# An attention and convolution kernel on one core: its order of work, planned by a scheduler or written out as a list

## The chip, the cores and the metric

The kernel runs on one core of a Trainium2 chip. The core has a matrix engine (PE, with a separate queue for loading weights, PEld), a vector engine (DVE), a scalar engine (ACT), a general engine (POOL) and a queue engine (SP) that here only issues DMA transfers. Each engine works through its own instruction list in order and waits on semaphores for the others. Products land in PSUM, eight banks of 128 partitions by 512 floats, and everything else lives in SBUF.

The metric is the device time of one execution, in microseconds (us), as the median of several runs. Before the change it is 368.91 us (three runs: 368.1, 368.91 and 369.94).

## The reference

The computation has two halves. The first is attention in which a query only sees keys of its own cluster: q, k and v have 4 batches, 8 heads, 768 rows of 64 columns, and each head has 16 centroids.

```python
q_assign = np.argmax(np.einsum('bhsd,hcd->bhsc', q_n, c_n), axis=-1)   # q_n, c_n: rows of length 1
k_assign = np.argmax(np.einsum('bhsd,hcd->bhsc', k_n, c_n), axis=-1)
mask = q_assign[:, :, :, None] == k_assign[:, :, None, :]
scores = np.where(mask, scale * np.matmul(q, k.transpose(0, 1, 3, 2)), -1000000000.0)
attn = np.exp(scores - np.max(scores, axis=-1, keepdims=True))
attn = attn / (np.sum(attn, axis=-1, keepdims=True) + 1e-09)
attn_out = np.matmul(attn, v)
```

Its output, with the heads side by side as x of 4 batches, 768 rows and 512 columns, goes through a gated long convolution:

```python
proj = x @ w_proj
x1, x2, x3 = (proj[..., :D], proj[..., D:2 * D], proj[..., 2 * D:])
x2_conv = np.fft.irfft(np.fft.rfft(x2, n=S, axis=1) * np.fft.rfft(filter_fft, n=S, axis=0)[None], n=S, axis=1)
return (x1 * x2_conv * x3) @ w_out
```

## The kernel before, in words

**Two steps: plan, then emit.** `build` first records the whole kernel as 1987 operations with `Plan.op`. An operation names the engines that may do it with a duration for each, a due time, the keys that it reads and writes (from which its dependencies follow), the PSUM bank that it opens (`alloc`) and those that it releases (`free`). Then `Plan.place` decides for every operation its engine, its place in time and its bank. Last, a loop at the end of the kernel function goes through the resulting list and calls each operation's function, which emits the instructions. So an engine's instruction list is the planned list, cut down to that engine.

**What the planner goes by.** `place` (L124 to L238) keeps for every engine the time at which it is free and its operations whose dependencies are placed. It takes the engine that can start earliest and on it, among the operations that could start within 0.1 us of the first, the one with the least due time. It models DMA rates (`RATE`), the exp table's load (`TABLE`) and a lock that keeps DVE and POOL from doing certain operations at once (`lock`). Two tables correct it by hand: `NUDGE` (L43) adds an offset to the due time of nearly every operation, and `ONLY` (L44) pins some operations to one engine. Banks come from `banks_for` (L241 to L263): those that are free earliest by the planner's clock, with at most four (`HELD`) held by scores and four by everything else while scores are open; banks 4 and 5 belong to the output of the attention.

**Attention.** A group is four heads of one batch, so there are eight groups, each with two pairs of heads (`attention(n, pr)`), and a pair has six key tiles of 128: 96 tiles in all. For one tile PE makes three score products into three banks (`sc`, L700, through `product` at L80), ACT takes exp of each into a buffer p (L714 and L717, five buffers), and PE multiplies p by v (`pv`, L728), adding into banks 4 and 5 over the six tiles. DVE adds up p over the tiles (`acc`, L741; the first two tiles with `part`, L737, on DVE or POOL) for the denominators. The mask needs no separate pass: q and k, in bfloat16 buffers `augs`, carry 16 extra rows with the one-hot word of the cluster, so the score product itself lowers the scores of other clusters. Casting q and k into `augs` (L633; the copy itself is at L283 for ACT, L285 for DVE and POOL) can be done by ACT, DVE or POOL.

**Routing.** `routing(n)` prepares a group while the one before is in its attention: PE transposes q and k (L627) or DVE does (L605), PE makes the similarities to the centroids (`sim`, L647), DVE finds the greatest and its word (L652 to L662), PE turns the words into hits with a triangular matrix `tri` (L667), ACT or DVE copies them to `ohT` (L673, L675), and SP moves them with eight DMAs into the extra rows of `augs` (`masks`, L512). For the first group, which has nothing to hide behind, `first_masks` (L517) writes the rows of one pair from PSUM directly (`put`, L564).

**Start.** Ahead of the first score stand the centroids' norms (a square root on ACT, L357, and a Newton step on DVE, L360 to L365), the filter's angles (sines on ACT), zero fills of `augs` (L1087 on ACT, or POOL), and the loads of q and k, which SP and ACT issue (L331).

**Convolution.** After the second group of a batch, `hyena(b)` runs on the batch's 768 rows beside the attention of the following groups; only the last batch's lies behind all attention. Its products on PE are the spectral input U (L855), the spectrum (L483), the gates G (L917), the inverse I (L946) and the output product W, with DVE, ACT and POOL in between.

**Shape of the array.** `product` (L80) makes a product either with the whole array, or as two matmuls on halves of 64 columns. `array(o, last)` (L59) says which shape an operation needs: pv and some others 64, small ones 32, and scores, gates and inverses take the shape that came last.

**The lock.** In the emission loop, an operation marked `lock` that goes to POOL waits for the last such operation that the loop has emitted for DVE:

```python
if o.lock and o.on == "POOL" and held:
    tc.add_manual_dep(traced[n], held[0].name, ...)
elif o.lock and o.on == "DVE":
    held = [traced[-1]]
```

## Time and profile before

| | |
|---|---|
| median of 3 runs | 368.91 us |
| span of the profiled execution | 367.2 us |
| PE busy | 354.3 us (96%) |
| DVE busy | 341.4 us (93%) |
| ACT busy | 264.3 us (72%) |
| POOL busy | 125.2 us (34%) |
| granted PE clock | 9 or more tenths in every slice |
| DMA | 46.20 MB, mean 126 GB/s |
| first pv starts | 26.39 us |
| last accumulation starts | 320.2 us |

The span is the stretch from the first to the last recorded instruction of one profiled execution; the profile gives no other time for that execution, and the median of the runs is 1.7 us longer than the span. "Busy" is the time in which an engine has an instruction in work; a matmul that waits in PE's pipe for its operands counts as busy. The chain of waits is the path that ends last: it starts at the last instruction and goes back, at each step, to what released it.

### The profile page before, as it was taken

How to read it: one execution, taken by the hardware profiler on the slowest of the kernel's cores; microseconds unless marked ns; L12 is line 12 of the kernel's file. 1: busy time of each engine (PE TensorE's matmuls, PEld its weight loads, DVE VectorE, ACT ScalarE, POOL GpSimd, SP SyncE). 2: the span in 40 equal slices, each digit the busy share in tenths (PEclk: the TensorE clock that was granted, in tenths of full speed). 3: DMA queues.
4: the chain of work that ended last, by engine and by line, in shares of the span. 5: the costliest groups of instructions: out<-in, count | busy, mean ns of one | idle time of the engine just before them, and what ended most of it. 6: DMA issues, size and time to landing. Idle time of an engine off the chain costs nothing.

```text
span 367.2 us, 8472 instructions
## 1 busy us (share of the span) xinstructions
PE 354.3 (96%) x3201; PEld 205.5 (56%) x3204; DVE 341.4 (93%) x455; ACT 264.3 (72%) x500; POOL 125.2 (34%) x152
## 2 busy tenths in 40 slices
PE   7799999999999999999999999989999999999995
PEld 3456455445655554655555655568655655656662
DVE  5999898999999989999999999999997999999984
ACT  4999997768986876879699774759965796234342
POOL 7510515322003556221310056424021433126750
PEclk9999999999999999999999999999999999999999
DMA  7866996585667986857777898554357631110124
GB/s 165 193 153 141 192 188 154 112 182 99 147 139 129 149 153 110 164 121 103 140 99 142 223 192 162 98 103 89 60 90 195 127 37 43 45 46 3 59 116 172
DMA packets 109797, 46.20 MB, mean 126 GB/s; under 512 B 97640, under 2 KB 103484, under 8 KB 109756
## 3 DMA queue, kind: packets, MB, share of 16 engines
q1 hardware_dynamic: 104556, 35.07, 43.1%
q0 software_dynamic: 2752, 8.98, 16.8%
q10 hardware_dynamic: 2448, 1.61, 1.4%
q8 instruction: 25, 0.41, 0.5%
q14 instruction: 16, 0.13, 0.1%
HBM read 31.59 MB, written 7.40 MB: 106 GB/s over the span
## 4 chain that ended last, share of the span: by engine, by line
PE 74%; DVE 9%; ACT 6%; DMA 5%; issue 2%; SPq 1%; ACTq 0%; DVEq 0%
PE bank L85 31%; PE pair L728 29%; PE bank L855 6%; DVE acc L741 2%; PE bank L627 2%; ACT p L717 2%; PE bank L647 2%; PE bank L83 2%; DMA y<-in_moe_filter_fft_dram 2%; DMA aug<-ohT 1%; DMA qkraw<-in_q_dram 1%; PE bank L490 1%; ACT aug L283 1%; DVE qkP L285 1%; DVE hm L470 1%
## 5 line engine op out<-in xcount | busy, mean ns | idle before, releaser
L728 PE MATMUL pair<-p,vraw 128*64 128x385 f32 x768 | 144.5, 489 | 0.8 <-ACT osb L744 0.3
L717 ACT ACTIVATE p<-bank 128x512 f32<-128x512 f32 x192 | 108.9, 607 | 23.7 <-PE bank L85 16.9
L741 DVE TENSOR_TENSOR acc<-p,acc 128x1536 f32<-128x1536 f32 x64 | 112.8, 1762 | 3.3 <-ACT p L717 0.6
L728 PEld LDWEIGHTS pair<-p,vraw 128*64 128x64 f32 x768 | 58.7, 136 | 45.2 <-issue 35.0
L85 PE MATMUL bank<-aug,aug 128*64 128x256 bf16 (+3 forms) x728 | 81.8, 327 | 1.6 <-ACT p L717 0.6
L85 PEld LDWEIGHTS <-aug 80*64 80x64 bf16 (+1 forms) x728 | 47.5, 109 | 38.0 <-issue 24.5
L714 ACT ACTIVATE p<-bank 128x512 f32<-128x512 f32 x96 | 57.7, 605 | 6.2 <-PE bank L85 4.1
L774 POOL DMA_DIRECT2D acc<-acc x30 | 23.7, 798 | 84.4 <-DVE acc L741 57.1
L285 POOL CAST aug<-qkP 64x768 bf16<-64x768 f32 x22 | 19.6, 894 | 74.8 <-DVE acc L741 52.1
L85 PE MATMUL bank<-xT,wpj 128*64 128x384 bf16 x456 | 43.5, 326 | 0.3 <-ACT ohT L673 0.2
L85 PEld LDWEIGHTS <-wpj 128*64 128x64 bf16 x456 | 28.1, 110 | 12.5 <-issue 3.8
L85 PEld LDWEIGHTS <-y 128*64 128x64 bf16 x472 | 24.4, 110 | 16.0 <-issue 6.0
L737 POOL TENSOR_TENSOR acc<-p,p 128x1536 f32<-128x1536 f32 x7 | 24.3, 3466 | 18.9 <-ACT p L717 9.5
L885 DVE TENSOR_TENSOR tm<-bank,hm 128x512 f32<-128x512 f32 x44 | 28.4, 684 | 2.3 <-PE bank L490 1.1
L283 ACT CAST aug<-qkP 64x768 bf16<-64x768 f32 x28 | 23.1, 831 | 3.9 <-DVE qkP L605 1.8
L85 PE MATMUL bank<-wout,y 128*64 128x512 bf16 (+1 forms) x200 | 24.3, 371 | 0.9 <-DVE y L977 0.4
L855 PE MATMUL bank<-wpj,xT 128*64 128x512 bf16 x192 | 22.5, 379 | 0.0
L283 ACT COPY ob<-bank 128x512 f32<-128x512 f32 x21 | 12.0, 591 | 12.4 <-PE bank L85 11.7
L889 POOL TENSOR_TENSOR y<-tm 128x512 bf16<-128x512 f32 x14 | 17.7, 1276 | 8.7 <-DVE tm L885 4.4
L283 ACT COPY qkP<-bank 128x384 f32<-128x384 f32 x36 | 16.5, 485 | 5.6 <-PE bank L647 2.1
L977 POOL TENSOR_TENSOR y<-yy,x 128x768 bf16<-128x768 f32 x6 | 10.9, 1824 | 24.6 <-DVE yy L972 12.6
L627 PE MATMUL bank<-ident,qkraw 128*128 128x128 f32 x120 | 18.8, 281 | 0.4 <-DMA qkraw<-in_k_dram 0.3
(182 smaller groups left out, 451.7 us busy)
## 6 DMA issues: line engine op xcount, KB each, us to landing
qkraw<-in_q_dram SPq DMA_DIRECT2D x30, 192.0 KB, 4.5
rb<-dr SPq DMA_DIRECT2D x30, 192.0 KB, 3.5
qkraw<-in_k_dram SPq DMA_DIRECT2D x51, 96.0 KB, 2.8
vraw<-in_v_dram SPq DMA_DIRECT2D x48, 96.0 KB, 3.2
out_dram<-ob SPq DMA_DIRECT2D x9, 512.0 KB, 3.7
acc<-acc POOLq DMA_DIRECT2D x10, 384.0 KB, 5.2
acc<-acc POOLq DMA_DIRECT2D x10, 192.0 KB, 4.0
vraw<-in_v_dram SPq DMA_DIRECT2D x4, 384.0 KB, 4.3
```

Source lines behind the costliest of these rows:

```text
L85: T.nc.tensor.matmul(out[64 * i:64 * i + 64], lhsT[:, 64 * i:64 * i + 64], rhs, start=start, stop=stop)
L283: T.nc.scalar.copy(out, in_)
L285: (T.nc.vector if e == "DVE" else T.nc.gpsimd).tensor_copy(out, in_)
L627: T.nc.tensor.transpose(ap(h)[:, ts(t, 128)], raw(s, 3 * ch + t), T.ident[:, ::-1] if ch > j else T.ident)
L714: T.nc.scalar.activation(o, ap(h).rearrange("p (a b) -> p a b", a=2), Act.Exp, scale=0.125)
L717: T.nc.scalar.activation(flat(s)[:, lo:lo + 512], ap(h), Act.Exp, scale=0.125)
L728: T.nc.tensor.matmul(o[64 * hp:64 * hp + 64, ch, :385], T.vraw[vs][:, hp, sk * D:(sk + 1) * D], T.p[slots[sk]][:, hp, 384 * ch:384 * ch + ...
L737: alu(e).tensor_tensor(T.acc[os], T.p[slots[0]][:, :, :S], T.p[slots[1]][:, :, :S], op=Alu.add)
L741: T.nc.vector.tensor_tensor(T.acc[os], T.p[slots[sk]][:, :, :S], T.acc[os], op=Alu.add)
L774: op(("POOL", .8), lambda e, rows=rows: T.nc.gpsimd.dma_start(flat_()[:rows], flat_()[rows:2 * rows], accum_op=Alu.add), te, r=[], w=AK, b ...
L855: T.nc.tensor.matmul(ap(h)[64 * i:64 * i + 64], T.xT[xs][:, kt, c:c + 64], T.wpj[:, kt, DM:2 * DM], start=kt == 0, stop=kt == ND - 1)
L885: op(("DVE", .68), lambda e, i=i, cs=cs, r=r, h=h: T.nc.vector.tensor_tensor(T.tm[r][:, cs], ap(h), hmrow(i, (0, 2, 2, 3)[2 * r + cs]), op ...
```

## The change

`NUDGE`, `ONLY`, `place`, `banks_for`, the heap import and the planner's constants are removed. In their place stands `ORDER`, a list of 1987 numbers: each is five times an operation's index plus the index of its engine in `ENGINES`. A new method `arrange` goes through the list. It asserts that every operation stands behind what it depends on, sets its engine, and gives it the PSUM banks that have been free longest (first in, first out), where before the planner gave those that it expected to be free earliest. The limit of four held banks is gone. Banks 4 and 5 stay with the attention's output while that runs, and may be taken by others before (class "head", until the first score) and after it. The recorded operations, the functions that emit them, the emission loop and the lock in it are the same. The list puts the operations in a different order on every engine and some of them on another engine:

| operations | PE | ACT | DVE | POOL | SP |
|---|---|---|---|---|---|
| before | 634 | 505 | 439 | 116 | 293 |
| after | 634 | 519 | 428 | 111 | 295 |

Among them are the casts into `augs` (ACT 28 to 37, DVE 14 to 8, POOL 22 to 19), the first addition of a pair `part` (POOL 7 to 5, DVE 9 to 11), one copy `put` of the first masks and two zero fills, which leave ACT. Neighbours in the list are not neighbours in time: runs of one engine's operations stand together. After the change a line of code has a number some 39 lower; the prediction uses the numbers of before.

```diff
-HELD = 4
 EARLY = 8.73655
-NUDGE = {0:3.939,1:2.28,2:2.825,
...
-ONLY = {15:"POOL",16:"ACT",17:"POOL",
...
+ENGINES = ['PE', 'ACT', 'DVE', 'POOL', 'SP']
+ORDER = [
+    2, 13, 48, 103, 23, 18, 28, 106, 199, 174, 194, 189, 154, 201, 51, 66, 181, 169, 179, 149, 159, 5, 112, 117, 37, 267, 62, 122, 207, 237, 242,
...
+]
...
-        o.due += NUDGE.get(o.seq, 0.0)
...
-    def place(self, free0, banks_for, switch=0.1, wait=0.1, rate=RATE, bonus=0.0, margin=0.02195, shape=0.0):
...
+    def arrange(self):
+
+        free, last, outs, done = [0, 1, 2, 3, 6, 7, 4, 5], None, 0, set()
+        tiles = sum(o.alloc is not None and o.alloc.cls == "o" for o in self.ops)
+        closed, scores, order = 0, 0, []
+        for x in ORDER:
+            o = self.ops[x // 5]
+            o.on = ENGINES[x % 5]
+            assert o.on in o.eng and o.deps <= done and o not in done
+            done.add(o)
+            order.append(o)
+            if o.alloc is not None:
+                if o.alloc.cls == "o":
+                    ids, outs = [4, 5], outs + 1
+                else:
+                    right = closed == tiles if outs else o.alloc.cls == "head" and not scores
+                    ids = [i for i in free if right or i not in (4, 5)][:o.alloc.n]
+                scores += o.alloc.cls == "score"
+                assert len(ids) == o.alloc.n and set(ids) <= set(free)
+                o.alloc.ids = tuple(ids)
+                free = [i for i in free if i not in ids]
+            if o.on == "PE":
+                mode = array(o, last)
+                last, o.whole = mode, mode == 128
             for h in o.free:
...
                 h.readers -= 1
...
                 if not h.readers:
...
+                    closed += h.cls == "o"
+                    free += h.ids
+        assert len(order) == len(self.ops)
+        return order
...
-def banks_for(bank, free, st, o):
...
-    order = P.place({"PE": .3, "ACT": .8, "DVE": .8, "POOL": .8, "SP": .8}, banks_for)
-    return P, order
+    return P, P.arrange()
```

More of the change, by code (lines that the diff above doesn't have):

```diff
@@ L2 @@
-import heapq
 import math
@@ L44 @@
-ONLY = {15:"POOL",16:"ACT",17:"POOL",30:"ACT",32:"SP",33:"SP",34:"SP",35:"SP",37:"SP",38:"SP",40:"SP",67:"ACT",69:"DVE",72:"DVE",73:"DVE",86:"DVE",91:"DVE",100:"POOL",101:"POOL",147:"ACT",149:"DVE",155:"DVE",159:"DVE",161:"DVE",176:"DVE",224:"DVE",225:"POOL",230:"DVE",231:"DVE",236:"POOL",237:"DVE",243:"DVE",251:"DVE",252:"DVE",254:"ACT",255:"DVE",325:"ACT",408:"POOL",411:"POOL",418:"POOL",420:"ACT",421:"POOL",503:"ACT",526:"ACT",531:"DVE",532:"DVE",533:"POOL",563:"DVE",571:"POOL",600:"DVE",701:"POOL",703:"POOL",706:"ACT",708:"ACT",710:"POOL",712:"DVE",873:"DVE",876:"ACT",879:"ACT",880:"POOL",884:"DVE",889:"POOL",901:"DVE",1033:"DVE",1042:"DVE",1071:"DVE",1072:"POOL",1085:"POOL",1087:"DVE",1096:"ACT",1099:"ACT",1167:"DVE",1169:"ACT",1171:"POOL",1174:"POOL",1179:"ACT",1183:"POOL",1355:"ACT",1356:"POOL",1358:"POOL",1461:"DVE",1514:"ACT",1525:"DVE",1526:"DVE",1555:"POOL",1559:"ACT",1561:"DVE",1569:"ACT",1641:"ACT",1644:"POOL",1649:"ACT",1650:"ACT",1859:"ACT",1865:"DVE",1896:"POOL",1904:"ACT",1917:"ACT",1920:"POOL",1922:"ACT",1924:"ACT",1925:"POOL",1935:"DVE",1939:"DVE",1949:"ACT",1953:"ACT",1964:"ACT",1967:"SP",1970:"ACT",1981:"ACT"}
+ENGINES = ['PE', 'ACT', 'DVE', 'POOL', 'SP']
@@ L45 @@
+ORDER = [
[82 rows of a table added]
+]
 THIRDS = [[(0, 0, 512)], [(0, 512, 768), (1, 0, 256)], [(1, 256, 768)]]
-HOLD = {"score": "score", "o": "o"}
-AFTER = {"PE": .16}
-TABLE = 1.283
 WARM = 10
-SOON = 0
-RATE = 215e3
 LOAD = 300e3
-COLD, SLOW = 6.0, .95
-OVERLAP = {"ACT": .09, "DVE": .08}
 MODES = {"pv": 64, "bc": 64, "half": 64, "sim": 32, "den": 32, "score": 0, "proj": 0, "inv": 0}
@@ L122, in op @@
         return o
-    def place(self, free0, banks_for, switch=0.1, wait=0.1, rate=RATE, bonus=0.0, margin=0.02195, shape=0.0):
-        free = dict(free0)
-        bank_free = [0.0] * 8
-        ready = {e: [] for e in free}
-        pend = 0
-        st = SimpleNamespace(pool=0.0, dve=0.0, bw={}, tab=None, last=None, kind=None, score=0, o=0, tail=0,
-                             held=dict(score=0, fill=0, o=0))
-        st.scores, st.otiles = (sum(o.alloc is not None and o.alloc.cls == c for o in self.ops) for c in ("score", "o"))
-        busy = dict.fromkeys(free, 0.0)
-        def enqueue(o):
-            o.ready = max([d.end - AFTER.get(d.on, 0.0) * (d in o.soft) + (0.06 if o.eng.keys().isdisjoint((d.on,)) or d.byts else 0.0)
-                           for d in o.deps] or [0.0])
-            if o.kind == "load":
-                o.ready = max(o.ready, o.due - LEAD)
-            for e in o.eng:
-                ready[e].append(o)
-        def take(o):
-            if o.alloc is None:
-                return
-            o.alloc.ids = banks_for(o.alloc, bank_free, st, o)[0]
-            for i in o.alloc.ids:
-                bank_free[i] = 1e9
-            st.score += o.alloc.cls == "score"
-            st.o += o.alloc.cls == "o"
-            st.held[HOLD.get(o.alloc.cls, "fill")] += o.alloc.n
-            if o.alloc.cls != "o":
-                st.tail |= st.o == st.otiles and any(i in (4, 5) for i in o.alloc.ids)
-        def done(o, e, t, d, end):
-            o.start, o.on = t, e
-            o.end = end + AFTER.get(e, 0.0)
-            if o.byts:
-                s, b = max(o.end + 1.3, st.bw.get(e, 0.0)), o.byts / rate
-                for f in [f for f in st.bw if f != e and st.bw[f] > s]:
-                    b += min(o.byts / rate, st.bw[f] - s)
-                    st.bw[f] += min(o.byts / rate, st.bw[f] - s)
-                st.bw[e] = s + b
-                o.end = st.bw[e] + 0.6 + o.lat
-            if e == "POOL" and o.lock:
-                st.pool = t + d
-            if e == "DVE" and o.lock:
-                st.dve = t + d
@@ L168, in done @@
             for h in o.free:
-                h.last = (e, o.end)
                 h.readers -= 1
-                h.end = max(h.end, o.end)
                 if not h.readers:
-                    st.held[HOLD.get(h.cls, "fill")] -= h.n
-                    for i in h.ids:
-                        bank_free[i] = h.end + 0.06
-            for x in o.eng:
-                ready[x].remove(o)
-            for x in o.outs:
-                x.left -= 1
-                if not x.left:
-                    enqueue(x)
@@ L183, in place @@
-        for o in self.ops:
-            if o.seq in ONLY:
-                o.eng = {ONLY[o.seq]: o.eng[ONLY[o.seq]]}
-        for o in self.ops:
-            if not o.left:
-                enqueue(o)
-        while any(ready.values()):
-            best = None
-            for e, lst in ready.items():
-                cand = []
-                for o in lst:
-                    f = free[e] + (TABLE if e == "ACT" and o.tab not in (None, st.tab) else 0.0)
-                    t = max(f, o.ready)
-                    m = margin if e == "PE" else 0.0
-                    late = max(f, o.ready + m)
-                    if o.alloc is not None:
-                        ids = banks_for(o.alloc, bank_free, st, o)
-                        if ids is None:
-                            continue
-                        t, late = max(t, ids[1]), max(late, ids[1] + m)
-                    for h in o.free:
-                        if h.last[0] not in (None, e):
-                            t, late = max(t, h.last[1] + 0.06), max(late, h.last[1] + 0.06)
-                    if o.lock and e in ("POOL", "DVE"):
-                        t = max(t, st.dve + 0.06 if e == "POOL" else st.pool)
-                        late = max(late, t)
-                    cand.append((late, o, t))
-                if not cand:
-                    continue
-                t0 = min(c[0] for c in cand)
-                c = min((c for c in cand if c[0] <= t0 + wait + 1e-9), key=lambda c: (
-                    c[1].due - (bonus if e == "PE" and st.kind == "pv" == c[1].kind else 0.0)
-                    + (shape if e == "PE" and array(c[1], st.last) != st.last else 0.0)
-                    + (BUSY if e == "DVE" and len(c[1].eng) > 1 else 0.0)
-                    + (c[0] - t0) * 0.2, c[1].seq))
-                if best is None or (t0, c[0]) < best[0]:
-                    best = ((t0, c[0]), e, c[1], c[2])
-            if best is None:
-                raise RuntimeError("stuck: " + repr([(e, [x.kind for x in l][:4]) for e, l in ready.items()]))
-            _, e, o, t = best
-            take(o)
-            d = o.eng[e]
-            if e == "ACT":
-                st.tab = o.tab or st.tab
-            if e == "PE":
-                d *= 1 + SLOW * (t < COLD)
-                mode = array(o, st.last)
-                if mode != st.last:
-                    d += switch
-                st.last, st.kind, o.whole = mode, o.kind, mode == 128
-            done(o, e, t, d, t + d)
-            busy[e] += d - OVERLAP.get(e, 0.0)
-            free[e] = t + d - OVERLAP.get(e, 0.0)
@@ L236, in place @@
-        self.busy = busy
-        self.span = max(o.end for o in self.ops)
-        return sorted(self.ops, key=lambda o: (o.start, o.seq))
-def banks_for(bank, free, st, o):
-    def whole(lo, hi):
-        return max(free[lo:hi])
-    if bank.cls == "o":
-        t = whole(4, 6)
-        return ((4, 5), t) if t < 1e8 else None
-    allowed, first = [0, 1, 2, 3, 6, 7], []
-    if st.score and st.score < st.scores:
-        if st.held["score" if bank.cls == "score" else "fill"] + bank.n > HELD:
-            return None
-    if st.o == 0:
-        allowed += [4, 5] if bank.cls == "head" and st.score <= SOON else []
-    elif st.o == st.otiles:
-        if st.tail:
-            allowed += [4, 5]
-        elif whole(4, 6) < 1e8:
-            first += [4, 5]
-    t = lambda i: whole(4, 6) if i in first else free[i]
-    ids = sorted((i for i in allowed + first if free[i] < 1e8), key=lambda i: (t(i), i))[:bank.n]
-    return (tuple(ids), max(map(t, ids))) if len(ids) == bank.n else None
+                    closed += h.cls == "o"
```

3 lines of the change are left out of this document (removed), and 81 rows, old and new, of the table ORDER.

## The prediction

> **What bounds the kernel now.** I read the engine shares first, then the chain of waits in order of time, then the timeline at the places where the chain leaves PE, and last the start.
>
> ```profile
> PE 354.3 (96%) x3201; PEld 205.5 (56%) x3204; DVE 341.4 (93%) x455; ACT 264.3 (72%) x500; POOL 125.2 (34%) x152
> PE 74%; DVE 9%; ACT 6%; DMA 5%; issue 2%; SPq 1%; ACTq 0%; DVEq 0%
> ```
>
> PE is busy for all but 12.9 us of the span of 367.2 us, and three quarters of the chain that ends last is PE. A busy share does not say whether PE runs at its pace, because a product that waits in the pipe counts as busy. So I take the price of each kind of product from the chain of waits (start, duration, what):
>
> ```profile
> 158.15 3.27 PE bank L85 x40
> 169.42 0.66 PE bank L85 x8
> 178.51 1.45 PE pair L728 x8
> 179.96 0.66 PE bank L85 x16
> 180.62 1.29 PE pair L728 x8
> 204.36 1.73 PE bank L855 x16
> 250.55 1.35 PE pair L728 x8
> ```
>
> In row order: five gate products G take 3.27, so 0.654 each, and each is four pairs of 384 columns, so 0.164 a pair; one tile's three score products take 0.66, so 0.22 each; an inverse product I takes 0.66; P times V (pv) takes 1.29; two spectral products U take 1.73, so 0.865, and an output product W has as many matmuls of the same width. The last row is used below. The pv at 178.51 takes 1.45, not 1.29: the product ahead of it used the whole array (its group's line is L83, not L85). I read 0.15 us for each change of array shape.
>
> With these prices I count the operations that stand between two pvs in the program's PE order and compare them with the time between their starts. In most of the span both agree within 0.1 us: PE never pauses there, and an order can win nothing. They disagree in two places, which the timeline shows:
>
> ```profile
> 180.45 1.47 PE L728 MATMUL pair<-p,vraw 128*64 128x385 f32 x8
> 189.47 1.68 PE L728 MATMUL pair<-p,vraw 128*64 128x385 f32 x7 [0.24 <-ACT p L717]
> 196.96 1.52 PE L728 MATMUL pair<-p,vraw 128*64 128x385 f32 x8
> ...
> 236.72 2.17 PE L728 MATMUL pair<-p,vraw 128*64 128x385 f32 x7
> 241.37 0.35 PE L85 MATMUL bank<-ohB,tri 128*64 128x384 bf16 x2 [0.69 <-ACT ohT L673]
> 242.36 5.98 SPq L512 DMA_DIRECT2D aug<-ohT  x8
> 247.30 0.41 PE L85 MATMUL bank<-aug,aug 80*64 80x512 bf16 x2 [0.31 <-DMA aug<-ohT]
> ```
>
> From 180.45 to 196.96 (pv 55 to pv 60, counted from 0) there are 16.5 us. Between them stand 5 pv, 21 scores, 3 W and 2 small pairs: 6.45 + 4.62 + 2.60 + 0.33 = 14.0. So 2.5 us are lost: these pvs wait for exps, and scores wait for banks that ACT has not emptied. From 236.72 to about 250.4 (pv 71 to 72, the latter the last row of the fence before) there are 13.7 us for 1 pv, 1 I, 10 G, 8 scores and 2 small pairs: 1.29 + 0.66 + 6.54 + 1.76 + 0.33 = 10.6. So 3.1 us are lost: SP needs 5.98 us to issue eight mask copies, and the first score of the next group waits for their landing. The same count from the first pv to the last leaves some 1 us more, in small pieces, mostly among the first 18 tiles. DVE (93%) is close behind PE, but the chain rarely goes through it after the start.
>
> The third piece is the start, before PE's saturated stretch:
>
> ```profile
> 2.91 4.11 DMA qkraw<-in_q_dram
> 7.04 0.40 ACTq L331
> 8.34 0.10 ACT s L357
> 9.43 0.26 DVE sd L365
> ```
>
> The four rows above are from the chain of waits. The next four are from the timeline (start, duration, engine, line, operation):
>
> ```profile
> 22.22 0.79 ACT L283 COPY aug<-bank 16x768 bf16<-16x768 bf16 x1
> 23.03 1.28 ACT L423 ACT_TABLE_LOAD   x1
> 24.55 1.09 ACT L717 ACTIVATE p<-bank 128x512 f32<-128x512 f32 x2
> 26.39 1.49 PE L728 MATMUL pair<-p,vraw 128*64 128x385 f32 x8
> ```
>
> ACT's third load stands until 7.04 for a q load that SP issued fourth (they share a completion semaphore). The square root of the centroid norms is queued behind it, then DVE's chain runs almost without a gap to the masks, ACT copies one mask itself, loads the exp table only then, and the first exp starts at 24.55.
>
> **The change, part by part.** The operations are the same 1987, so PE's products cost the same. What is left is: where PE changes shape, what each queue has ahead of the critical operation, and how far a producer stands from its reader.
>
> *Array shapes.* Between first and last pv the old PE order changes shape 45 times, the new one 34 times (start 8 and 8, tail 4 and 4). 11 x 0.15 = 1.65 us less, all on PE's path. Products that move between one whole-array matmul and two half ones are costed at nothing: a few of 634 change.
>
> *Start.* In the new order ACT's third load shares its semaphore with the k half that SP issues second. SP's issues stand 0.5 to 0.9 us apart, so that one lands one to two issues sooner, and the square root comes right behind it, without the 0.83 us zero fill that stood between. The root can then run at about 6.3. DVE's own list reaches the Newton step at about 7.4 (it stands until 3.04 for the centroids, then has some 4.3 us of work), where before the step began at 8.46: 1.1 us sooner. Behind it, to the last mask copy, the DVE list loses one 0.56 us cast and moves some angle work, and gains the mask copy that ACT had (0.56). On ACT the 0.79 us copy is gone from the front of the 1.28 us table load. What is late next is the routing product of group 1 (1.46 us on PE ahead of the first score), which waits for ACT's copies. Summed by rows I get the first exp at about 22.9, not 24.55: 1.7 us. Bounds: 0, if those copies come as late as now, and 2.6, if only DVE counts.
>
> *Scores and exps.* For each pv I sum the PE work listed between the last score of its tile and the pv. Before, eight of 96 have under 1.6 us (the shortest, 0.65, at pv 58; four of the eight are pv 56, 58, 59 and 47), median 5.6. After, two have (1.08 both, pv 0 and pv 24; before, pv 24 also had 1.08 and lost nothing), the next has 1.95, median 6.3. So the cause of the 2.5 us is thinned out. ACT's backlog there can stay in part: I take 1.9 saved, bounds 0 and 2.5.
>
> *Masks.* Between the routing words' last product and the first score that needs the masks the old order puts 4.5 us of PE work at the group of the 3.1 us stall. By the rows that stretch took 5.9 us (241.37 to 247.30). The new order puts 7.1 us there, its smallest value in any group (old: 4.5, 5.2, 7.1 and more). The work covers the stretch with 1.2 us to spare. I take 2.8 saved, bounds 0 and 3.1. If DVE or ACT is late by more than that spare, the stall returns at that size.
>
> *Work between engines.* ACT takes 519 operations (505), among them 37 casts of the kind below (28); DVE 428 (439); POOL 111 (116), with five 3.46 us adds for seven.
>
> ```profile
> L283 ACT CAST aug<-qkP 64x768 bf16<-64x768 f32 x28 | 23.1, 831 | 3.9 <-DVE qkP L605 1.8 <-PE bank L85 1.8
> L737 POOL TENSOR_TENSOR acc<-p,p x7: 3461/3464/3475, 55.5 to 305.0; 128x1536 f32<-128x1536 f32 x7
> ```
>
> Nine casts are 7.5 us more on an engine that is idle 28% of the span. I cost it at nothing, where it falls in idle time; where it does not, it is in the next item.
>
> *New waits.* Every order has places of its own that no row of the old trace shows. The nearest measure is what the old one has in all after its first pv: 2.5 + 3.1 + 1 = 6.6 us. Bounds 0 and 6.6, and no gain, as nothing negative can come from a wait. I take 1.5, near the 1 us that is lost now in places without a short distance.
>
> *Tail.* After the last pv PE works through the same kinds of products without a gap worth naming, and two copies and stores follow its end. Both orders end in the same operations. Nothing taken.
>
> Sum: -1.7 - 1.65 - 1.9 - 2.8 + 1.5 = -6.55. The profiled span of 367.2 becomes 360.6. The median run, 368.91, is 1.7 us longer than that span, which I keep: **362.4 us**.
>
> **Rivals.**
> *The waits move.* The shorter start and the fewer shapes stay, but stalls of the same sum appear elsewhere, for instance at the masks of another group. For it: banks go to the longest free, not the earliest expected. Against it: both distances above grew everywhere. -3.35 gives 365.6.
>
> *ACT comes too late (slower).* The window rows (time, then busy of PE, PEld, DVE and ACT) show that ACT is already full for whole stretches, one of them the stretch of the 2.5 us loss:
>
> ```profile
> 10.00:20.00 10.00, 8.27 (x61) 5.05 (x59) 9.54 (x22) 9.80 (x20) 5.26 (x16) 1.00 0.88 217
> 190.00:200.00 10.00, 9.81 (x86) 6.03 (x86) 9.69 (x12) 9.99 (x19) 0.58 (x1) 1.00 0.70 127
> ```
>
> If 7.5 us of casts and 5 us of small copies fell into such stretches, exps would be late by up to 12 us. From 6.6 us on this eats the gain; at 10 us it gives 372. Against it: ACT idles over 20% in most other windows.
>
> *DVE stands for POOL.* An accumulation of the old trace began 0.43 us before the end of a POOL operation (timeline); the last row gives its line's minimum, median and maximum in ns.
>
> ```profile
> 253.80 1.82 POOL L977 TENSOR_TENSOR y<-yy,x 128x768 bf16<-128x768 f32 x1 [4.14 <-DVE acc L737]
> ...
> 255.19 2.05 DVE L741 TENSOR_TENSOR acc<-p,acc 128x1536 f32<-128x1536 f32 x1 [0.61 <-ACT p L717]
> ```
>
> ```profile
> L741 DVE TENSOR_TENSOR acc<-p,acc x64: 1695/1757/2194, 32.1 to 320.2; 128x1536 f32<-128x1536 f32 x64
> ```
>
> It took 0.29 us over the median; the longest of the line is 0.44 over. If the new order lets accumulations fall under the 3.46 us adds, each can cost up to that; two cost 6.9 and give 369.3, five give 380. Against it: behind the operation that each add waits for, DVE's list has 2.9 to 7.3 us of work before the next operation of that kind, as before. [...]
>
> *No change.* The gains cancel against new waits: 368.9.
>
> **How the numbers follow.** Forecast 0.59; the waits move 0.19; ACT too late 0.12; port 0.05; no change 0.05. 0.5% is 1.8 us, about what a measurement of this kernel can tell from no change. The first two end below 367.1, so faster is 0.78; no change and part of the port case give same 0.08; slower 0.14. All bounds in favour (2.6 + 1.65 + 2.5 + 3.1 + 0.9) reach 358.2; the forecast's own range is 358.2 to 365, and to leave out no more than 2 in 10 the range goes up to 369.4.
>
> **What would show it.** Right: first pv at 24 to 25.5; about 47 shape changes; a wait of under 0.5 us on the mask copies near the seventh group; time between pv starts equal to listed work at pv 55 to 60. Wrong: a first pv at 26 or later; ACT over 9.9 of 10 us in more than four windows with PE under 9.8; accumulations over 3 us; SP waits that end in a score.

## The result, and the profile after

The changed kernel takes 364.8 us (median of 4 runs, 363.23 to 366.35) against 369.09 before on the same chip: a ratio of 0.989, with an interval of 0.985 to 0.993. In a later set of runs it was 367.5 against 370.1, a ratio of 0.990 (0.986 to 0.994). So it is faster by 1.0 to 1.1%. The medians are over all executions, while the ratios leave out those over 1.5% above the kernel's fastest (of the later set two, 369.0 and 369.3), so a ratio is not the quotient of the two medians beside it. The profiled execution took 363.86 us, with a span of 362.1.

The page of the changed kernel has the engine shares and the chain nearly as before, with 5 us less of PE:

```profile
PE 349.1 (96%) x3197; PEld 200.6 (55%) x3200; DVE 335.0 (93%) x444; ACT 271.4 (75%) x516; POOL 113.0 (31%) x147
PE 75%; DVE 8%; ACT 7%; DMA 6%; issue 2%; SPq 1%; DVEq 0%; ACTq 0%
```

The start, from the timeline (start, duration, engine, line, operation, idle time before it and its releaser): the square root of the norms, the load of the exp table, the first exp, the first pv.

```profile
5.92 0.20 ACT L319 ACTIVATE s<-ss 128x1 f32<-128x1 f32 x1 [1.79 <-DVE kp L1016]
20.52 1.28 ACT L385 ACT_TABLE_LOAD   x1
22.38 1.28 ACT L679 ACTIVATE p<-bank 128x512 f32<-128x512 f32 x2 [0.36 <-PE bank L157]
24.42 1.49 PE L690 MATMUL pair<-p,vraw 128*64 128x385 f32 x8
```

The root runs at 5.9 instead of 8.3, the exp table is there before the first score, and the first pv starts 2.0 us sooner. The two places of the prediction, again from the timeline: pv 55 and pv 60, then pv 71, the first two thirds of the next group's first scores, and pv 72.

```profile
181.05 1.46 PE L690 MATMUL pair<-p,vraw 128*64 128x385 f32 x8
195.23 1.14 PE L690 MATMUL pair<-p,vraw 128*64 128x385 f32 x6
```

```profile
239.45 1.49 PE L690 MATMUL pair<-p,vraw 128*64 128x385 f32 x8
242.69 0.41 PE L157 MATMUL bank<-aug,aug 80*64 80x512 bf16 x2
244.47 0.52 PE L157 MATMUL bank<-aug,aug 128*64 128x256 bf16 x4 [0.60 <-DMA aug<-ohT]
246.75 1.49 PE L690 MATMUL pair<-p,vraw 128*64 128x385 f32 x8
```

From pv 55 to pv 60 there are 14.2 us for 13.9 us of listed work and two changes of shape: the loss of 2.5 us is gone. From pv 71 to pv 72 there are 7.3 us for 1 pv, 5 gate products and 9 scores, 6.5 us: of the 3.1 us, 0.8 are left, and 0.6 of them are a wait of the *second* score for its masks. But a new loss stands early, in group 1 (the copy of a denominator, DMAs on SP's queue, PE):

```profile
49.06 0.62 SPq L728 DMA_DIRECT2D dd<-den  x1
51.48 1.52 PE L690 MATMUL pair<-p,vraw 128*64 128x385 f32 x8
57.37 0.49 ACT L722 ACTIVATE den<-bank 128x384 f32<-128x384 f32 x1 [3.53 <-DMA dd<-den]
57.91 0.41 PE L157 MATMUL bank<-aug,aug 80*64 80x512 bf16 x2 [2.89 <-ACT den L722]
61.23 1.16 PE L690 MATMUL pair<-p,vraw 128*64 128x385 f32 x6
```

All pairs of heads share one tile `den`. The DMA that reads the first pair's denominators was issued at 49.06 and landed after 57.3; the copy of the second pair's stands in ACT's list where ACT reaches it at 53.8, so ACT waits 3.5 us, and PE idles 2.9. From pv 11 (51.48) to pv 13 (61.23) 4.1 us are lost. Before, the two copies stood 16 us apart and nothing waited for that DMA.

A smaller new loss stands at pv 24, the first of group 2: 1.3 us, where the old order lost 0.4. PE waits there for an accumulation on DVE before the products that make the denominators; in the old order a transposition stood between.

```profile
87.39 0.85 PE L716 MATMUL bank<-acc,ones 128*32 128x384 f32 x8 [0.70 <-DVE acc L703]
```

| part of the span | predicted | measured |
|---|---|---|
| start, to the first pv | -1.7 | -2.0 (26.39 to 24.42) |
| changes of shape | -1.65 | -1.2 (an estimate: 11 at 0.11, see below) |
| pv 55 to 60 | -1.9 | -2.5 |
| pv 71 to 72 | -2.8 | -2.3 |
| new waits | +1.5 | +4.0 (what the other rows leave) |
| work moved behind the last pv | 0 | -1.1 |
| sum | -6.55 | -5.1 (367.2 to 362.1) |

The last row but one: 1.4 us of listed products stand behind the last pv now and not ahead of it, yet the stretch behind it grew by only 0.3 us.

### The profile page after: what moved, and what is told of

Read it like the earlier page. It is cut to its first block, busy times and chain, and to the rows that moved or that the text cites. A ratio compares the mean times of both kernels' runs of the same rounds, so it can differ in the third digit from the quotient of the medians.

```text
span 362.1 us, 8441 instructions
## 1 busy us (share of the span) xinstructions
PE 349.1 (96%) x3197; PEld 200.6 (55%) x3200; DVE 335.0 (93%) x444; ACT 271.4 (75%) x516; POOL 113.0 (31%) x147
## 4 chain that ended last, share of the span: by engine, by line
PE 75%; DVE 8%; ACT 7%; DMA 6%; issue 2%; SPq 1%; DVEq 0%; ACTq 0%
PE bank L157 31%; PE pair L690 28%; PE bank L817 6%; PE bank L155 2%; PE bank L589 2%; DMA dd<-den 2%; ACT p L679 2%; PE bank L609 2%; ACT p L676 2%; DMA aug<-ohT 1%; ACT aug L245 1%; DMA qkraw<-in_k_dram 1%; ACT ohT L635 1%; DMA qkraw<-in_q_dram 1%; DVE qkP L567 1%
## 5 line engine op out<-in xcount | busy, mean ns | idle before, releaser
L690 PE MATMUL pair<-p,vraw 128*64 128x385 f32 x768 | 142.1, 488 | 0.3 <-ACT osb L706 0.3
L157 PE MATMUL bank<-aug,aug 80*64 80x512 bf16 (+3 forms) x724 | 81.6, 326 | 4.8 <-ACT den L722 2.9
L690 PEld LDWEIGHTS pair<-p,vraw 128*64 128x64 f32 x768 | 55.8, 136 | 44.2 <-issue 35.9
L157 PEld LDWEIGHTS <-aug 80*64 80x64 bf16 (+1 forms) x724 | 44.5, 109 | 44.7 <-issue 31.2
L247 POOL CAST aug<-qkP 64x768 bf16<-64x768 f32 x19 | 15.6, 820 | 52.2 <-DVE acc L703 22.3
L245 ACT CAST aug<-qkP 64x768 bf16<-64x768 f32 x37 | 30.6, 828 | 0.6
L245 ACT COPY qkP<-bank 128x384 f32<-128x384 f32 x41 | 18.5, 485 | 8.7 <-PE bank L157 5.4
L939 POOL TENSOR_TENSOR y<-yy,x 128x768 bf16<-128x768 f32 x7 | 12.7, 1821 | 30.9 <-DVE yy L934 27.8
L699 POOL TENSOR_TENSOR acc<-p,p 128x1536 f32<-128x1536 f32 x5 | 17.3, 3465 | 6.7 <-ACT osb L706 4.0
L699 DVE TENSOR_TENSOR acc<-p,p 128x1536 f32<-128x1536 f32 x11 | 19.1, 1740 | 0.0
```

The lines of the kernel that those rows point to most:

```text
L157: T.nc.tensor.matmul(out[64 * i:64 * i + 64], lhsT[:, 64 * i:64 * i + 64], rhs, start=start, stop=stop)
L245: T.nc.scalar.copy(out, in_)
L690: T.nc.tensor.matmul(o[64 * hp:64 * hp + 64, ch, :385], T.vraw[vs][:, hp, sk * D:(sk + 1) * D], T.p[slots[sk]][:, hp, 384 * ch:384 * ch + ...
L699: alu(e).tensor_tensor(T.acc[os], T.p[slots[0]][:, :, :S], T.p[slots[1]][:, :, :S], op=Alu.add)
```

## The experiments

Kernels of the changed form have the list `ORDER`; "the order of before as the list" has the same list filled with the order and engines that the planner gave. "Lost" is time between two pv starts less their listed work. A line of code has another number in each of these kernels. A kernel that is given with one time and no ratio (old_masks, old_cast, put_act, no_lock) has a single execution and is read by its rows.

### The rule for banks and the start alone

```diff
-ORDER = [  # old_list: the order of the changed kernel
+ORDER = [  # old_list: all 1987 in the order and on the engines of before
...
+ORDER = [  # new_start: the 181 operations that the planner placed before 26 us as in the changed kernel, then the rest as before
```

> The order and the engines of before, written out as the list, with the banks given first in, first out (389 of 546 bank choices differ from before). Theory (the gain is in the order, the rule for banks is worth nothing): 369.1 within 1.5 us, first pv at 26.4, the same losses of 2.5 us at pv 55 to 60 and 3.1 us at pv 72. Rival (banks that are free longest shorten or lengthen the waits): over 2 us from 369.1, with the difference at the scores.

> The list of the changed kernel for the 181 operations of the start (those that the planner placed before 26 us), and the order of before for all others. Theory (the start is worth its 2.0 us whatever follows): first pv at 24.4 and all later pvs 2.0 us sooner than before, 367.1. Rival (the loads that later work needs come no sooner, so the lead is lost behind the start): first pv at 24.4, but under 1 us left at pv 24, 368.5 or more.

The first and the last pv of old_list, then those of new_start with one more row:

```profile
26.55 0.84 PE L675 MATMUL pair<-p,vraw 128*64 128x385 f32 x4
320.12 1.47 PE L675 MATMUL pair<-p,vraw 128*64 128x385 f32 x8
```

```profile
24.10 1.49 PE L675 MATMUL pair<-p,vraw 128*64 128x385 f32 x8
318.03 1.47 PE L675 MATMUL pair<-p,vraw 128*64 128x385 f32 x8
328.86 1.48 PE L802 MATMUL bank<-wpj,xT 128*64 128x512 bf16 x11 [0.88 <-DVE xT L767]
```

The order of before with the new bank rule takes what before takes: 369.8, a ratio of 1.001 (0.998 to 1.004), with the same losses at the same pvs. So the rule for banks is worth nothing here, and the whole gain is in the order. The start alone gives 368.2, a ratio of 0.9965 (0.9935 to 0.9994). Of its 2.4 us, 2.1 are there at the last pv (320.12 to 318.03), but the spans (367.9 and 367.0) differ by only 0.9: 1.2 us go behind the last pv, 0.9 of them in a wait of PE for DVE that old_list does not have. The theory held up to the last pv, and about half of its gain was lost after it.

### The price of a change of shape

```diff
+FORCE = {...}  # 59 scores, between two pvs at 21 places
...
-                mode = array(o, last)
+                mode = 128 if o.seq in FORCE else array(o, last)
```

> The changed kernel with the scores between two pvs made by the whole array at 21 places (59 score products) where nothing waits, which makes 42 more changes of shape. Theory of the prediction (0.15 us a change): 6.3 us more than the changed kernel, 0.30 us at each place. Rival (what the two traces give, where places with two changes of shape lose some 0.15 us less than priced, so 0.07 to 0.08 us a change): 2.9 to 3.4 us more, 0.15 us at each place.

Two neighbouring pvs (57 and 58) of the changed kernel, and the same two here, with the three scores between them made by the whole array:

```profile
186.13 1.47 PE L690 MATMUL pair<-p,vraw 128*64 128x385 f32 x8
187.87 1.46 PE L690 MATMUL pair<-p,vraw 128*64 128x385 f32 x8
```

```profile
189.26 1.52 PE L691 MATMUL pair<-p,vraw 128*64 128x385 f32 x8
191.25 1.19 PE L691 MATMUL pair<-p,vraw 128*64 128x385 f32 x6
```

1.74 became 1.99: two changes cost 0.25 here. The 21 places have 0.18 to 0.26, on average 0.22. So a change cost 0.11 us in this run, halfway between the 0.15 of the prediction and the 0.075 of the rival: the term was right in kind and a third too dear. These are changes between the whole array and halves of 64 columns. Of the 11 changes that the new order saves, 8 are to or from the whole array; the other 3 are between products on 64 and on 32 columns, which this run does not price. The run took 370.3 us (ratio 1.000, 0.997 to 1.004): 42 changes cost as much as the whole change had won.

### The wait on the denominator

```diff
-            h, den_, dk = Bank(), lambda: T.den, ["den"]
+            h, den_, dk = Bank(), lambda: T.den, ["den"]
+            if pr and n < FIRST:
+                den_, dk = lambda: T.x3[1][:, 0], [("x3", 1, 0)]
```

> The changed kernel; the denominators of the second pair of groups 0 and 1 go to a buffer that is free then, instead of the one tile that all pairs share. Nothing else is different. Theory (the copy of the second denominator waits until the DMA that reads the first one has landed, and everything behind it on ACT waits with it): the ACT wait of 3.5 us and the PE idle of 2.9 us at 54 to 58 are gone, pv 12 starts within 0.6 us of its listed work, and the run is 3.4 to 4.1 us under the changed kernel's 364.8: about 361. Rival (ACT or SP is behind there anyway, and the wait only hides it): PE idles at the same place for another reason and the run is within 1 us of 364.8.

The wait for `den` is gone: pv 12 starts at 55.5, not 58.1. But the run took 365.4 us (ratio 0.988, 0.985 to 0.992), no less than the changed kernel, and its last pv started at 315.1, 1.4 us later. The rival was right about the time, and nearly about the reason: another wait stood behind it, with PE idle some 12 us later and not at the same place. The rows of DVE and PE, and then windows of 1 us (time, busy of PE, PEld, DVE, ACT and POOL, the granted clock of PE, the share of the DMA engines, GB/s):

```profile
60.58 0.98 DVE L567 STREAM_TRANSPOSE qkP<-qkraw 128x768 f32<-128x768 f32 x1 [2.52 <-DMA vraw<-in_v_dram]
69.77 0.55 PE L589 MATMUL bank<-ident,qkraw 128*128 128x128 f32 x3 [1.57 <-DVE hm L432]
```

```profile
40.00:60.00 20.00, 19.45 (x156) 9.64 (x154) 17.46 (x17) 16.83 (x33) 8.70 (x9) 1.00 1.04 201
```

```profile
70.00:71.00 1.00, 1.00 (x7) 0.42 (x7) 1.00 (x2) 0.48 (x1) 0.00 (x0) 0.92 0.94 148
71.00:72.00 1.00, 1.00 (x6) 0.43 (x4) 1.00 (x1) 0.00 (x0) 0.00 (x0) 0.50 0.84 207
...
74.00:75.00 1.00, 1.00 (x16) 0.26 (x12) 0.14 (x2) 1.00 (x3) 0.91 (x2) 0.88 0.88 159
```

DVE stands until 60.6 for loads, and the DMA engines are full from 40 to 60 us (a share of 1.04); the accumulations queue up behind the transposition, and PE idles 1.6 us at 68 to 70. Then something that no step of the prediction had: from 70.8 to 74.2 PE's clock is half (0.50 in the windows), which costs another 1.7 us by an estimate (half of 3.4 us).

The next kernel lets DVE transpose that load later:

```diff
 # den2_k: den2, and on DVE
-... 419 (transpose of the second k), 365 (acc), 214, 373 (acc), 420 (cast), 381 (acc) ...
+... 365 (acc), 214, 373 (acc), 419 (transpose of the second k), 420 (cast), 381 (acc) ...
```

> The kernel with the second denominator buffer (den2), where DVE transposes the second k half of group 2 behind two accumulations instead of ahead of them. Theory (with the wait on the denominator gone, DVE reaches that transposition at 57.5, waits until 60.6 for a k load, because the DMA engines are full from 40 to 61 us, and its accumulations stand behind it): the DVE wait is gone, PE's idle of 1.6 us at 68 to 70 and the 1.5 us after it are gone, and the last pv starts 3 us or more sooner than in den2 (315.1): about 312; ratio to before about 0.98. Rival (loads set the pace up to 61 us for other readers too): another wait of 2 us or more takes its place before pv 24, and the last pv stays over 314.

```profile
61.13 0.97 DVE L552 STREAM_TRANSPOSE qkP<-qkraw 128x768 f32<-128x768 f32 x1
312.55 1.46 PE L675 MATMUL pair<-p,vraw 128*64 128x385 f32 x8
```

The transposition no longer waits, and in the profiled execution, 362.7 us, the last pv starts 2.5 us sooner than in den2, somewhat less than the 3 us of the theory; between two executions of the changed kernel that place differs by more (313.6 and 317.1). The median is 366.7 us nevertheless (ratio 0.9905, 0.9874 to 0.9935): no gain over the changed kernel. The next run tells part of why.

### The changed kernel once more

> The changed kernel once more, beside the version above on the same chip. Expected: 0.989 of before within 0.003. Theory (the wait of 2.9 us at 54 to 58 varies with the DMAs, and PE's clock is halved for some 3 us behind it in some executions): executions with a mean clock under 0.996 take 2 us or more longer than those over it. Rival (the spread is of the loads alone): no such tie.

The same stretch in its profiled execution, DVE and PE, and three windows:

```profile
59.24 0.98 DVE L567 STREAM_TRANSPOSE qkP<-qkraw 128x768 f32<-128x768 f32 x1 [2.66 <-DMA qkraw<-in_k_dram]
...
60.91 0.63 PE L157 MATMUL bank<-aug,aug 80*64 80x256 bf16 x6 [3.27 <-DVE hm L432]
```

```profile
62.00:63.00 1.00, 1.00 (x6) 0.52 (x4) 1.00 (x1) 0.98 (x3) 0.00 (x0) 0.50 0.00 0
63.00:64.00 1.00, 1.00 (x7) 0.40 (x5) 1.00 (x3) 0.00 (x0) 0.00 (x0) 0.50 0.00 0
64.00:65.00 1.00, 1.00 (x10) 0.83 (x8) 1.00 (x1) 0.44 (x1) 0.00 (x0) 0.50 0.16 14
```

This execution lost nothing to `den` (0.6 us up to pv 12) and 4.9 us right behind it, where DVE waits for a k load and PE for DVE; then the clock is half for over 3 us (0.50 in the windows from 62 to 65). So the wait at 54 to 61 us has no single owner: whichever of the operations placed there needs a late transfer first is the one that waits. Of 12 executions of the changed kernel that the comparisons use, 4 had a mean clock of 0.996 or more and took 363.5 us on average; 8 were below and took 367.0. Before, 61 of 67 were at 0.996 or more, at 369.6 us. The expectation's tie is there: 3.5 us. It does not show what is cause and what is effect. One stretch of 3.4 us at half clock costs only half of that by the estimate above (under den2), so the other executions must lose more, in the pause itself or in a second such stretch; the two traces have one execution of each kind.

### The masks before pv 72

```diff
 # old_masks: the order of before as the list, and on PE
-... 1075 (G), 1573 (score 1), 1077 (G), 1079 (G), 1575 (score 2) ...
+... 1075 (G), 1077 (G), 1079 (G), 1573 (score 1), 1575 (score 2) ...
 # and on ACT
-... 1063, 1574 (exp of score 1), 1074 (copy of a gate product) ...
+... 1063, 1074 (copy of a gate product), 1574 (exp of score 1) ...
 # old_cast: the order of before as the list, and on ACT
-... 1640, 1641, 1436 (exp), 1643, 1646, 1439, 1052, 1368, 1367, 1048, 1370, 1371 (hits) ...
+... 1436 (exp), 1646, 1439, 1052, 1368, 1367, 1048, 1370, 1371 (hits), 1640, 1641, 1643 (casts of group 7) ...
```

> The order of before as the list, with one change: the first score of group 6 stands behind two more gate products (1.3 us), so that 5.8 us of products and not 4.5 stand between the words and that score. Theory (the stall at pv 72 is the masks' 5.9 us less the work that covers them): the loss at pv 72 falls by 1.3 us, from 3.1 to 1.8. Rival (SP's issues or ACT set the place in time, whatever PE does): the loss stays within 0.4 us of 3.1.

```profile
249.25 0.52 PE L142 MATMUL bank<-aug,aug 80*64 80x512 bf16 x4
...
250.61 1.61 PE L142 MATMUL bank<-aug,aug 128*64 128x256 bf16 x18 [0.84 <-DMA aug<-ohT]
```

The theory fell: 3.6 us were lost, not 1.8, and the run took 370.1 us. With the score its exp moved too, behind a copy on ACT, which the expectation does not name. The first score waits for nothing; the second one, which needs the copies for the other half, waits until 250.6, and the two gate products had stood between them anyway.

> The order of before as the list, with three casts of group 7 on ACT, which nothing needs soon, moved behind the hits of group 6. Theory (the loss at pv 72 comes from ACT's queue: the exp of pv 71 and the hits stand behind 2.5 us of casts, and the masks follow the hits): hits and masks end 2 us or more sooner, and the loss at pv 72 falls from 3.1 to 1.2 or less. Rival (the products listed between words and score decide): the loss stays over 2.5.

```profile
240.99 0.99 ACT L620 ACTIVATE ohT<-bank 64x384 bf16<-64x384 f32 x2
```

```profile
243.51 3.44 PE L142 MATMUL bank<-xT,wpj 128*64 128x384 bf16 x40 [0.64 <-DVE sd L909]
...
249.12 1.61 PE L142 MATMUL bank<-aug,aug 128*64 128x256 bf16 x18 [0.40 <-DMA aug<-ohT]
```

The hits end at 242.0, 2.0 us sooner than in old_list (243.95), as expected, but the second score starts only 0.9 us sooner (249.12 for 250.03), 3.3 us are lost, and PE waits for DVE instead. That theory fell too. The run took 369.0 us. What the new order does there to win 2.3 us stays open. The last hits before, and the hits after the change:

```profile
241.85 1.00 ACT L673 ACTIVATE ohT<-bank 64x384 bf16<-64x384 f32 x2
```

```profile
235.54 1.73 ACT L635 ACTIVATE ohT<-bank 64x384 bf16<-64x384 f32 x4
```

The old order has the hits done 6 us behind the start of pv 71 (236.72), the new one at 237.3, 2 us ahead of it (239.45), with DVE, ACT and SP all shifted. old_cast moved them by 2 of these 8 us, so whether much earlier hits are the cause is neither shown nor ruled out.

### A mask copy back on ACT

```diff
 # put_act: the changed kernel
-... 85 (copy of a mask row) on DVE
+... 51, 85 (copy of a mask row) on ACT, 61 (load of the exp table) ...
```

> The changed kernel with one copy of the first masks put back on ACT, ahead of the load of the exp table, as before. Theory (ACT's copy stands in the way of the table and the first exp): the first exp starts at 22.8 instead of 22.4 and the first pv 0.4 us later. Rival (DVE's chain alone sets the start, and it loses a copy of 0.55): the first score and the first pv come 0.3 to 0.5 us sooner.

```profile
20.73 0.79 ACT L230 COPY aug<-bank 16x768 bf16<-16x768 bf16 x1
21.54 1.28 ACT L370 ACT_TABLE_LOAD   x1
23.18 1.29 ACT L664 ACTIVATE p<-bank 128x512 f32<-128x512 f32 x2
```

The first exp came at 23.2 and the first pv at 25.2, both 0.8 us later (expected 0.4). In the eight other traces with the changed kernel's start the first pv comes at 24.1 to 24.9, so the loss is 0.3 to 1.1 us. That fits a copy that costs its full length on ACT, as the start's step had it; DVE's next copy also had to wait for it, 1.1 us. The run took 365.0 us.

### The lock between DVE and POOL

```diff
-        if o.lock and o.on == "POOL" and held:
+        if False:
```

> The changed kernel without the wait of POOL for DVE's last operation of the same kind (the lock; no data hangs on it). Theory of the third rival (an accumulation under a POOL add stands for the rest of the add): single accumulations on DVE take over 3 us, POOL starts its adds and casts sooner, and the last pv comes 2 us or more later. Rival (both run side by side): no accumulation over 2.2 us, and the last pv within 1 us of 313.6 or sooner.

The line of the accumulations (minimum, median and maximum in ns) in the changed kernel, and then without the lock:

```profile
L703 DVE TENSOR_TENSOR acc<-p,acc x64: 1694/1758/1910, 29.7 to 312.6; 128x1536 f32<-128x1536 f32 x64
```

```profile
L703 DVE TENSOR_TENSOR acc<-p,acc x64: 1696/1758/6508, 29.6 to 331.3; 128x1536 f32<-128x1536 f32 x64
```

382.9 us, 18 more than with the lock. Three accumulations take 3.3, 5.0 and 6.5 us, and by the pages POOL's casts into `augs` take 1.12 us on average for 0.82 with the lock, its additions 3.70 for 3.46; behind the longest accumulation PE stands for 4.5 us. So the price that the third rival (port in its list of chances) named is there. In the changed kernel, where the lock holds POOL back, it isn't paid: the longest accumulation is 1.9 us. What POOL's waits for the lock cost there was not measured.

### A version of both orders

```diff
 # tri95, tri85: three parts of the list
+ORDER = [  # the start (181 operations) of the changed kernel;
+           # the order of before for what the planner placed before 95 us (tri95) or 85 us (tri85);
+           # the order of the changed kernel for all else
```

> The list of the changed kernel for the start (as in new_start), the order of before up to what the planner placed before 95 us (past pv 24), and the list of the changed kernel for all else. Theory (the losses of each stretch belong to its order and add up): first pv at 24.1 to 24.4, 2.6 to 3.0 us lost up to pv 24 (with 0.075 us a change of shape taken off), 2.8 us lost after it; the last pv starts at 310.6 to 311.2, 2.4 to 3.0 us sooner than in the changed kernel; ratio to before about 0.981. Rival (waits move: what is won before pv 24 is lost again behind it): the last pv at 313 or later.

```profile
104.40 6.29 DMA rb<-dr
```

tri95 took 367.0 us (ratio 0.993, 0.989 to 0.996): 5.2 us were lost at pv 32, behind the seam, where the load of the reciprocals landed late (the row is from its chain of waits, at 110.7). The products behind it ran slower: by the same chain 16 of them took 2.91 us from 112.92, and 24 took 2.59 us from 116.98; the mean clock of this execution is 0.995. Neither theory nor rival is settled by it.

> As tri95, but the order of before ends at 85 us of the planner: there both lists have done the same operations on PE, ACT and DVE (none out of place; at 95 us 28 of ACT's were). Theory (the losses of each stretch belong to its order; tri95 lost 5 us at its seam, because two unlike ACT lists met there): no loss over 1.5 us between pv 23 and pv 32, the last pv at 310.6 to 311.8, ratio to before 0.977 to 0.983, and most executions at a full clock, since no idle of PE over 1.5 us is left. Rival (waits move whatever the seam): the last pv at 313 or later, ratio 0.988 or more.

```profile
89.94 1.51 PE L675 MATMUL pair<-p,vraw 128*64 128x385 f32 x8
112.93 1.46 PE L675 MATMUL pair<-p,vraw 128*64 128x385 f32 x8
314.26 1.46 PE L675 MATMUL pair<-p,vraw 128*64 128x385 f32 x8
```

tri85 took 364.4 us, a ratio of 0.986 (0.982 to 0.990); the changed kernel on the same chip took 367.5, with 0.990 (0.986 to 0.994). The seam is clean: 0.4 us lost from pv 24 (89.94) to pv 32 (112.93). All six executions had a clock of 0.996 or more. In the profiled one, however, 2.0 us went at pv 12 to 14 and 1.1 at pv 34, so its last pv was no sooner than the changed kernel's 313.6, against the expectation of 310.6 to 311.8. It has the best median of all, 3 us under the changed kernel on that chip, but the intervals overlap, and the path is no shorter: its six executions take 364.5 on average, and the changed kernel's four at a clock of 0.996 or more 363.5 (the two of them on that chip as well). What it has is that no execution shows the lower clock.

## Why the prediction was right, and where it was not

The direction and the range were right: 364.8 lies between the forecast of 362.4 and the rival in which the waits move (365.6), and nearer to the latter. As ratios to before, the forecast is 0.982 and that rival 0.991; the intervals of both sets (0.985 to 0.993 and 0.986 to 0.994) take in the rival and not the forecast. So the forecast itself was 2.4 to 2.8 us too low, and the range held because it was drawn wide enough for the rivals.

*Start.* Right, -2.0 for -1.7. new_start has it alone; put_act gives the mask copy on ACT 0.8 of it, within 0.3 to 1.1. What the step did not see is that half of it can be lost behind the last pv.

*Array shapes.* Right in kind; 0.11 a change instead of 0.15, so 1.2 instead of 1.65. The step counted all 11 changes at the price of one kind; with the 8 that the run prices alone it is 0.9, and 0.3 less is left for the new waits.

*Scores and exps.* Right, and more than was taken: 2.5 of 2.5. The traces show the loss gone; no run isolates the cause. pv 24, which the step set aside because it had lost nothing at the same distance, did lose 1.3 us, but through DVE and not through an exp.

*Masks.* The amount came out (-2.3 for -2.8), the reasoning did not. The step put the loss of 3.1 us down to the first score's wait for masks and priced it by the products ahead of that score. Its own rows said less: the wait was 0.31 us, and an ACT wait of 0.69 and a pv of 2.17 us stood beside it. old_masks and old_cast show that neither more products ahead of the first score nor hits 2 us earlier bring the gain. Its cause stays open.

*New waits.* This is the step that failed: +1.5 was taken, +4.0 came, as much as the loss of 4.1 us at pv 11 to 13 alone. The step had said that no row of the old trace shows the new places. One could have been found in the two lists: by the durations that the kernel gives its operations, ACT has 14.5 us of work from one copy into `den` to the next in the old order and 4.2 us in the new, and in the old trace the DMA between them landed 8.5 us after its issue. But den2, without this wait, was not faster: the late loads of that stretch stop the next reader (DVE, 2.5 us), so the tile alone is not the cause.

*Tail.* Costed at nothing; the work moved behind the last pv gave 1.1, and no run isolates it.

*Rivals.* The waits moved in part: stalls of some 6.5 us in the old order and 6 in the new, by the prediction's own prices between first and last pv. "ACT too late" did not come: the place where ACT stopped PE is a wait on a DMA, not too much work. The third rival's price is there in no_lock, its case did not come: the lock is in both kernels. That an accumulation could lose up to an addition's 3.46 us was an estimate from one row of before (0.43 us of overlap, 0.29 us more); in no_lock the three longest lost 1.5, 3.3 and 4.8 us over the median of 1.76.

*The median.* The forecast kept the distance of the median from the span. For executions at full clock that fits: 363.5 after against 369.6 before, 6.1 us less, near the forecast's 6.5. The median holds less: after the change more executions have a mean clock under 0.996 (8 of 12, before 6 of 67), and those took 367.0 us on average.

## What to carry to other kernels

When an order is changed, list for every tile that is written twice the distance from its readers, DMAs above all, to the next write: a tile that was far enough apart in the old order may be the first wait of the new one. In den2, where the DMA engines were full from 40 to 60 us (a share of 1.04), the wait of 3.5 us for `den` was gone and DVE waited 2.5 us for a late load: such a stretch is judged by what must arrive, not by its largest wait. And read a wait from the row that waits: a loss between two points is not the wait that is easiest to see between them.

## What the runs showed of the hardware that was not expected

A pause of PE was followed by a further loss in two runs. In den2 PE idled 1.6 us up to 69.77, in after_again 3.3 us up to 60.91; by the windows of 1 us the granted clock then fell from 1.00 to 0.50, some 1 us after PE had begun again, and was back at 1.00 some 3.4 us later (70.8 to 74.2 and 61.8 to 65.3), 1.7 us of lost work each by an estimate (half of 3.4). no_lock had a pause of 4.5 us up to 55.15, and its page shows 7 and 8 tenths of the clock in the two slices from 47.6 to 66.7 us. In the first profile of the changed kernel a pause of 2.9 us (up to 57.91) had no such effect: its windows from 54 to 62 us all have a clock of 1.00. So the length of the pause alone does not say whether the clock falls; what does was not shown. Mean clocks of 0.988 to 0.995 over an execution are what one to three such stretches make, by an estimate (half of 3.4 us is 0.5% of the span), and the executions of the changed kernel that have them take 2 to 4 us longer. Why den2_k, at 0.998 in its profiled execution, is below 0.996 in seven of nine executions was not seen, since each set of executions has one trace.
